# A gated S4 convolution kernel: weight products taken in the loaded layout and turned as sums, the lag rearrangement in 16 wider matmuls, residual matrices on GpSimd, and a new order of the work

## The chip, the core and the metric

The kernel runs on one core of one Trainium2 chip. TensorE (PE), VectorE (DVE), ScalarE (ACT), GpSimd (POOL) and SyncE (SP, which issues most of the DMAs) run side by side, each through its own instructions in a fixed order, and wait for one another through semaphores. The metric is the device time of one execution in microseconds; the time shown for a kernel is the median of its runs.

## What is computed

`A_u` is a sequence of 2048 tokens by 512 channels. Three things are done with it and mixed: a long convolution with a kernel that is a sum of 128 damped exponentials per channel (branch a), a small feed-forward network applied to the two tokens that a router picks (branch b), and a gate per token.

```python
def reference(...):
    def _A_ref(u, A_re, A_im, B_re, B_im, C_re, C_im, log_dt, Dskip):
        dt = jnp.exp(log_dt)[:, None]
        logdA = dt * (A_re + 1j * A_im)
        dB = dt * (B_re + 1j * B_im)
        l = jnp.arange(L).astype(bfloat16)                       # lags, rounded to bf16
        P = jnp.exp(logdA[:, :, None] * l[None, None, :])
        K = jnp.einsum("dn,dnl,dn->dl", C_re + 1j * C_im, P, dB).real
        y = irfft(rfft(K padded to 2 L) * rfft(u padded to 2 L))[:L]
        return y + u * Dskip
    def _B_ref(x, w_r, w_gate, w_up, w_down):
        idx = two tokens with the largest x @ w_r
        y = ((silu(x[idx] @ w_gate) * (x[idx] @ w_up)) @ w_down) * sigmoid(x[idx] @ w_r)
        return x with y added at the rows idx
    g = sigmoid((A_u * gate_w).sum(-1, keepdims=True))
    return g * _A_ref(A_u, ...) + (1 - g) * _B_ref(A_u, ...)
```

The weight of each exponential is the complex product C·B·dt. The parameter matrices are 512 channels by 128 exponentials (`N`).

## The kernel before

Nothing loops at run time: the program writes out some 570 steps, and each step has a name (`"kmm"`, `"sel"`, ...), one or more engines that it may run on (its *alternatives*, with a cost that the author's planner assumes), the buffers it reads and writes, and a number in the order in which it was written down. `PLAN` is a list of (step number, alternative) that fixes by hand which engine takes a step and the order on each engine; `BANKS` does the same for the places of the 83 PSUM tiles. `emit_plan` derives the semaphore waits. So an engine that waits for one step holds up everything behind it in its own list.

The 512 channels are worked on as two halves `hf` = 0, 1 (called `c` in later stages) of 256. The stages, with the names used below:

- **Weights.** Six parameter matrices are loaded as `NAT` (`nat0` to `nat5`), each with the channels in groups of four on the 128 partitions. `turned` (line 505) turns a matrix with four matmuls, so that the exponentials lie on the partitions: `nt0`, `nt1` for A, `nt2` to `nt5` for B and C. `cce` copies the turned C out of PSUM. `w1`, `w2`, `wr`, `wi` form the real and imaginary part of C·B, and `kw` multiplies by dt. `k0` sums `kw` for lag 0.
- **Coarse and fine factors.** Every lag is a sum of a coarse and a fine part. `ep` and `eq` are 256-wide exponentials on ACT (line 401), `pa` computes angles on PE (lines 578, 579), `arg` computes others on DVE or ACT (lines 559, 560), `sin` evaluates them on ACT, and `ns`, `pi`, `pr` (coarse) and `px` to `qr` (fine, `group`, line 794) multiply on DVE. The exponentials of half 0 that run first need only `al`.
- **Transform.** `fw` (line 724) multiplies the input tokens `U` (two loads of 1 MB, `u0`, `u1`) with Fourier matrices `FM`; `fwe` and `fwo` evict from PSUM, `vb` combines.
- **Lags** (line 842). `kmm` (line 853): 128 small matmuls per half give the convolution kernel at all lags; `kae` evicts them into `KA`. `sel` (line 868) brings the lags into the order that the next stage needs, as a product with selection matrices, 32 rows of output at a time, and `kce` evicts that into `KC`.
- **Spectrum** (line 874). `ks` (lines 886 to 891) multiplies `KC` with Fourier matrices, `khe` evicts; `i` = 0 is the near part of the lags, `i` = 1 the far part. Four tiles of `ks` per half and part, two PSUM banks each.
- **Products** (line 908). `prod`, `acc`, `yr`, `yi`, `pq` on DVE multiply the two spectra, for half `c` and output block `j`. For `c` = 0, `j` = 1 the sums are taken on PE instead (`ac`, line 936), which reads four `prod` results.
- **Inverse** (line 963). `iv` (lines 990, 993) transforms back and accumulates, per tile one matmul with a residual matrix `RD` that brings in branch b, `ive` multiplies by the gate on the way out of PSUM, and `out` stores.
- **Rows.** `log` gives router and gate values. The gate goes through the chain `sge` (ACT), `sgd` (POOL), `sgr` (DVE), `sgo`, `gf`, `gc`, `omg` (POOL); `rrec` (DVE) and `rr` (POOL) form (1 - g) / g per token, and `rd` (line 1043) multiplies the identity by it: eight 128x128 diagonal matrices per output block. `sc` (POOL) scatters the two rows of branch b into a copy of the input, and `ue` and `u2` load that copy back.

`TT` (line 375) is the helper of nearly all DVE products, `EV` (line 397) that of the evictions (ACT line 392 or DVE line 398), `AF` that of ACT functions (line 401).

Of the kernel before, what the change touches and what calls it, by code (L numbers as in the profile page):

```python
# [1121 lines left out]
```

## Time and profile before

| | us |
|---|---|
| median of 3 runs | 169.33 |
| lowest, highest run | 169.23, 172.55 |
| the profiled execution's own time | 168.66 |
| its span, first to last instruction | 166.9 |

The mean granted clock of TensorE was 0.98. The profile has a page with the busy time of each engine, the span in 40 slices, the chain of work that ended last and the costliest groups, and its trace can be asked for the instructions in order of time (the timeline: start, duration, engine, line, operation, output and input, number merged, idle time before and what ended it) and for busy times by window.

### The profile page before, as it was taken

The numbers are of one execution on the slowest core, as the hardware profiler recorded it, in microseconds if no ns is written. First come the engines' busy times: TensorE is split into PE (matmuls) and PEld (weight loads), VectorE is DVE, ScalarE is ACT, GpSimd is POOL, SyncE is SP. The second block draws the span as 40 slices with busy tenths as digits, with TensorE's granted clock in tenths as the row PEclk, the third lists the DMA queues.
The fourth block names the chain that finished last, engine by engine and source line by source line (L and its number), as shares of the span: only waits on it lengthen the run. The fifth ranks groups of instructions, "written<-read, shape, count | busy, mean of one in ns | idle before, by whom it ended". The sixth has DMA issues, their size and how long they took to land.

```text
span 166.9 us, 3538 instructions
## 1 busy us (share of the span) xinstructions
PE 149.1 (89%) x1483; PEld 108.0 (65%) x1491; DVE 146.0 (88%) x172; ACT 129.9 (78%) x243; POOL 17.9 (11%) x27
## 2 busy tenths in 40 slices
PE   1738998999999999999946899999999999999993
PEld 0523475666684685575633778768886785887882
DVE  0598899999998997898899999899897989999952
ACT  4599988999999999998999899698477360443432
POOL 6000000116005580000000042000000000000000
PEclk9975999999999999999999999999999999999999
DMA  3899999990009900001891000979300004001226
GB/s 113 300 356 230 265 389 374 415 377 18 1 9 335 602 4 0 4 0 29 277 401 51 2 4 24 338 298 370 110 0 0 4 0 126 0 4 55 70 70 181
DMA packets 21330, 25.89 MB, mean 155 GB/s; under 512 B 9118, under 2 KB 17188, under 8 KB 20644
## 3 DMA queue, kind: packets, MB, share of 16 engines
q1 hardware_dynamic: 21042, 25.55, 46.0%
q8 instruction: 11, 0.18, 0.4%
q10 hardware_dynamic: 146, 0.13, 0.2%
q0 software_dynamic: 128, 0.01, 0.2%
q14 instruction: 3, 0.02, 0.0%
HBM read 21.49 MB, written 4.20 MB: 154 GB/s over the span
## 4 chain that ended last, share of the span: by engine, by line
PE 62%; ACT 21%; DVE 7%; DMA 6%; SPq 2%; issue 1%
PE psm L993 17%; PE psm L724 12%; ACT RB L401 11%; PE psm L886 6%; ACT RB L392 6%; DVE RB L376 6%; DMA RB<-in_A_u_dram 6%; PE psm L936 4%; PE psm L853 3%; PE psm L578 3%; PE psm L579 3%; ACT L401 2%; PE psm L990 2%; PE psm L890 2%; PE psm L891 2%; PE psm L868 2%
## 5 line engine op out<-in xcount | busy, mean ns | idle before, releaser
L376 DVE TENSOR_TENSOR RB<-RB 128x2048 bf16<-128x2048 bf16 (+6 forms) x119 | 121.7, 1059 | 5.2 <-ACT RB L392 1.9
L392 ACT ACTIVATE RB<-psm 128x1024 bf16<-128x1024 f32 (+7 forms) x46 | 39.9, 908 | 12.3 <-PE psm L936 5.5
L401 ACT ACTIVATE RB<-RB 128x256 bf16<-128x256 f32 (+3 forms) x111 | 41.1, 452 | 2.3 <-DVE RB L376 2.3
L724 PE MATMUL psm<-RB 128*128 128x512 bf16 x121 | 31.7, 395 | 1.3 <-DMA RB<-in_A_u_dram 0.5
L993 PE MATMUL psm<-RB 128*128 128x256 bf16 x256 | 31.7, 273 | 0.0
L993 PEld LDWEIGHTS psm<-RB 128*128 128x128 bf16 x256 | 25.0, 98 | 3.1
L1007 ACT ACTIVATE RB<-psm,RB 128x256 bf16<-128x256 f32 x27 | 11.3, 472 | 16.6 <-PE psm L993 16.6
L401 ACT ACTIVATE RB<-psm 128x1024 bf16<-128x1024 int16 (+2 forms) x25 | 22.2, 936 | 0.6 <-PE psm L579 0.5
L724 PEld LDWEIGHTS psm<-RB 128*128 128x128 bf16 x128 | 12.6, 101 | 15.4 <-issue 2.2
L579 PE MATMUL psm<-RB 128*128 128x256 f16 x88 | 18.2, 273 | 0.3 <-ACT RB L401 0.3
L886 PE MATMUL psm<-RB 128*128 128x256 bf16 x128 | 16.3, 273 | 0.3 <-ACT RB L392 0.3
L578 PE MATMUL psm<-RB 128*128 128x256 f16 x88 | 15.0, 273 | 0.3 <-ACT RB L392 0.3
L853 PE MATMUL psm<-RB 128*128 128x80 bf16 x256 | 12.3, 199 | 2.5 <-ACT RB L392 1.6
L886 PEld LDWEIGHTS psm<-RB 128*128 128x128 bf16 x128 | 12.4, 98 | 2.1 <-ACT RB L392 0.6
L853 PEld LDWEIGHTS psm<-RB 128*128 128x128 bf16 x256 | 10.2, 97 | 4.9 <-PE psm L853 2.5
L401 ACT ACT_TABLE_LOAD x7 | 9.0, 1283 | 1.8 <-PEq L1107 1.7
L509 PE MATMUL psm<-RB 128*128 128x128 bf16 x24 | 5.4, 454 | 5.2 <-DMA RB<-in_A_B_re_dram 3.5
L578 PEld LDWEIGHTS psm<-RB 128*128 128x128 f16 x88 | 8.4, 98 | 2.5 <-ACT RB L392 0.4
L579 PEld LDWEIGHTS psm<-RB 128*128 128x128 f16 x88 | 8.2, 98 | 2.5 <-ACT RB L401 0.9
L398 DVE CAST RB<-psm 128x1024 bf16<-128x1024 f32 (+1 forms) x7 | 8.2, 1191 | 1.6 <-PE psm L853 1.1
L727 PE MATMUL psm<-RB 128*128 128x512 bf16 x31 | 9.3, 379 | 0.1
L990 PE MATMUL psm<-RB 128*128 128x256 bf16 x32 | 8.7, 273 | 0.2 <-issue 0.2
(64 smaller groups left out, 123.4 us busy)
## 6 DMA issues: line engine op xcount, KB each, us to landing
RB<-c_fwd SPq DMA_DIRECT2D x2, 1024.0 KB, 6.5
RB<-in_A_u_dram SPq DMA_DIRECT2D x2, 1024.0 KB, 9.4
RB<-c_near SPq DMA_DIRECT2D x2, 1024.0 KB, 5.1
RB<-c_inv SPq DMA_DIRECT2D x1, 2048.0 KB, 8.3
RB<-u_routed SPq DMA_DIRECT2D x2, 1024.0 KB, 6.8
RB<-in_B_w_gate_dram SPq DMA_DIRECT2D x1, 1792.0 KB, 9.9
RB<-in_B_w_up_dram SPq DMA_DIRECT2D x1, 1792.0 KB, 10.2
RB<-in_B_w_down_dram SPq DMA_DIRECT2D x1, 1792.0 KB, 7.5
```

Source lines behind the costliest of these rows:

```text
L376: return P.add(name, [(eng, c_dve(n, mode) if eng == DVE else 1.6, lambda h: h.tensor_tensor(out=o(), in0=a_(), in1=b_(), op=op))], rd, wr ...
L392: return lambda h: h.activation(out=o(), in_=a_(), func=ACTF.Copy, scale=scale() if callable(scale) else scale)
L401: return P.add(name, [(ACT, cost or c_act(n), lambda h: h.activation(out=o(), in_=a_(), func=func, scale=scale))], rd, wr, table=table, **kw)
L578: h.matmul(o, DGM(0, 128, (DPE.index(d) + 2) * 128, (1, 128)), HL(0, 128, k * 512 + c0, (1, w)), start=(k == 0 and i * w % 512 == 0), stop ...
L579: r = h.matmul(o, DGM(0, 128, 0, (1, 128)), DGM(0, 128, 128 + 1 - cs, (0, w)), start=False, stop=(cs == 0), skip_group_check=True)
L724: r = h.matmul(P32(t, k2, 0, 128, 0, (1, 512)), FM(0, 128, pl * 4096 + (par * 4 + q) * 512 + (2 * kp + k2) * 128, (1, 128)), U(0, 128, ((m ...
L727: r = h.matmul(P32(t, k2, 0, 128, 0, (1, 512)), CI(0, 128, 128 if pl == 1 - par * hc else 256, (1, 128)), V(0, 128, vo[0][2 * kp + k2] + ( ...
L853: x = h.matmul(P32(t, q // 6, 0, 128, (q % 6) * 80, (1, 80)), TPv(0, 128, ri * 16384 + c * 8192 + r * 128, (1, 128)), TQv(0, 128, c * 1024 ...
L886: x = h.matmul(o, KN(0, 128, g * 2048 + col, (1, 128)), KC[c](0, 128, g * 256, (1, 256)), start=(g == 0), stop=(g == NG - 1 and pl == 1))
L990: h.matmul(o, RD(0, 128, (tb + 8) % 16 * 128, (1, 128)), UE[qp](0, 128, (q2 * 2 + par) * 256, (1, 256)) if early else U2(0, 128, tb * D + ...
L993: x = h.matmul(o, G(0, 128, (pl * 4 + k0_ + kt) * 1024 + (par * 4 + q) * 128, (1, 128)), PQ(0, 128, 2048 * par + (k0_ + kt) * 512 + pl * 2 ...
L1007: r = h.activation(out=OT[k](0, 128, (4 * qp + 2 * q2 + par) * 256, (1, 256)), in_=P32(t, 0, 0, 128, q2 * 256, (1, 256)), func=ACTF.Copy, ...
```

## The change

- The turns `nt2` to `nt5` and `cce` go. `w1`, `w2` multiply the loaded bf16 matrices directly, `wr`, `wi` follow, and the two float32 sums are turned by eight transposes, a new PE step `wt`, into a two-bank PSUM tile that `kw` reads. `wt` needs the float32 identity `cf`.
- `sel` writes four PSUM banks, one for each remainder `c4`, each with all 320 columns in order, in 16 matmuls instead of 48; `kce` puts the order right as it reads: its innermost step goes from bank to bank.
- `rd` gets a third alternative, one GpSimd multiplication with an assumed cost of 4.5, and the plan takes it for both output blocks. Before, ACT made both.
- `PLAN` and `BANKS` are new throughout. SP's order becomes `nat5, cia, nat1, nat3, nat2, nat4, dgb, cf, dga, dsr, u0, fm, xt` (before: `cia, nat1, nat4, dga, nat3, nat5, fm, nat2, u0, xt, dgb, cf, dsr`). PE runs 24 `pa` matmuls and `wt` ahead of the first `fw`. Of the `arg` steps six go from ACT to DVE and one from DVE to ACT. From DVE to ACT go one `fwe`, one `fwo` and two wide `kae` of half 0; from ACT to DVE one `fwe`, one `ns` and the narrow `kae` of half 1. The gate's chain from `sge` to `rr`, which ran beside the coarse and fine stages, comes after `sc` on POOL, with `sge` on ACT among the evictions of the first spectrum and `rrec` on DVE behind the `yr` of the first products. `iv` of the first block, which stood in part between `sel` of half 1 and the second spectrum, comes wholly behind the first `ac`. On PE `zt` moves ahead of `sel` of half 0, and on DVE `bu` behind the last fine product. A few assumed latencies and priorities of loads, which only the planner reads, are changed as well.

```diff
-PLAN = [(0, 0), (4, 0), (5, 0), (3, 0), (6, 0), (1, 0), (23, 0), (29, 0), (225, 0), (2, 0), (13, 0), (7, 0), (180, 0), (22, 0), (244, 0), (207, 0), (243, 0),
...
+PLAN = [(0, 0), (14, 0), (3, 0), (4, 0), (5, 0), (1, 0), (23, 0), (6, 0), (24, 0), (234, 0), (242, 0), (240, 0), (203, 0), (2, 0), (22, 0), (25, 0), (26, 0),
...
-tB, tC = P.pst(2, "tb"), P.pst(2, "tc")
-for i in range(4):
-    turned(2 + i, (tB, tC)[i // 2], i % 2)
-CC = at("TP", 58880, 2048, BF); bCC = bf_("cc", "TP", 58880, 2048)
-EV("cce", row(CC, 0, 1024), lambda: P32(tC, 0, 0, 128, 0, (1, 1024)), [tC], [bCC], 1024)
...
-TT("w1", row(W1, 0, 1024), pq_(tB, 0, 1024), row(CC, 0, 1024), ALU.mult, [tB, bCC], [bW1], 1024, 1)
+TT("w1", row(W1, 0, 1024), lambda: NAT(0, 128, 1024, (1, 1024)), lambda: NAT(0, 128, 2048, (1, 1024)), ALU.mult, bNAT[2:], [bW1], 1024, 1)
...
+tW = P.pst(2, "tw")
+def wt(h):
+    r = None
+    for i, w in enumerate((W1, W2)):
+        for db in range(4):
+            r = h.transpose(P32(tW, i, 0, 128, db, (4, 128)), w(0, 128, db * 128, (1, 128)), CF(0, 128, 0, (1, 128)))
+    return r
+MM("wt", wt, [bW1, bW2, bCF], [tW], 2.0)
-TT("kw", row(KW, 0, 1024), lambda: W12(0, 128, 0, (1024, 2), (1, 512)), lambda: DTB(0, 128, 0, (0, 2), (1, 512)), ALU.mult, [bW1, bW2, bDTB], [bKW], 1024, 1)
+TT("kw", row(KW, 0, 1024), lambda: P32(tW, 0, 0, 128, 0, (1, 1024)), lambda: DTB(0, 128, 0, (0, 2), (1, 512)), ALU.mult, [tW, bDTB], [bKW], 1024, 1)
...
-t = P.pst(3, "sel")
+t = P.pst(4, "sel")
...
-    for jp in range(3):
-        nj = 2 if jp < 2 else 1
-        for c4 in range(4):
-            for g in range(4):
-                x = h.matmul(P32(t, jp, 32 * g, 32, c4, (256, nj), (4, 64)), CI(0, 128, 384 + 32 * c4, (1, 32)),
-                             KA[c](0, 128, (8 * jp + g) * 4 + c4, (16, nj), (80, 64)), start=True, stop=True, tile_position=(0, 32 * g))
+    for c4 in range(4):
+        for g in range(4):
+            x = h.matmul(P32(t, c4, 32 * g, 32, 0, (1, 320)), CI(0, 128, 384 + 32 * c4, (1, 32)),
+                         KA[c](0, 128, 4 * g + c4, (16, 5), (80, 64)), start=True, stop=True, tile_position=(0, 32 * g))
...
-EV("kce", lambda: KC[c](0, 128, 0, (1, 1280)), lambda t=t: P32(t, 0, 0, 128, 0, (1, 1280)), [t], [bKC[c]], 1280)
+EV("kce", lambda: KC[c](0, 128, 0, (256, 5), (4, 64), (1, 4)), lambda t=t: P32(t, 0, 0, 128, 0, (64, 5), (1, 64), (512, 4)), [t], [bKC[c]], 1280)
...
-             (ACT, 2.4, rd_act)], [bCIA, bSGF["rr"]], [bRD[j]])
+             (ACT, 2.9, rd_act), (POOL, 4.5, lambda h: h.tensor_tensor(out=RD(0, 128, (8 - 8 * j) * 128, (128, 8), (1, 128)), in0=CI(0, 128, 0, (0, 8), (1, 128)), in1=SGF["rr"](0, 128, 8 * j, (1, 8), (0, 128)), op=ALU.mult))], [bCIA, bSGF["rr"]], [bRD[j]])
```

15 lines of the change are left out of this document (7 added, 8 removed), and 74 rows, old and new, of the table PLAN.

## The prediction

> **What bounds the kernel now.** I read the page's busy times first, then its 40 slices, then busy times by window, and last the timeline of each engine around the hand-overs that these show.
>
> ```profile
> span 166.9 us, 3538 instructions
> PE 149.1 (89%) x1483; PEld 108.0 (65%) x1491; DVE 146.0 (88%) x172; ACT 129.9 (78%) x243; POOL 17.9 (11%) x27
> ...
> PE   1738998999999999999946899999999999999993
> ...
> DVE  0598899999998997898899999899897989999952
> ACT  4599988999999999998999899698477360443432
> ```
>
> No engine has much room, so the question is which of them sets the pace in which stage. PE dips in slices 21 and 22 only, ACT is full until about slice 25, and DVE is nearly full throughout.
>
> ```profile
> 5.86:92.30 86.44, 76.19 (x767) 48.36 (x773) 80.00 (x109) 84.45 (x164) 12.39 (x18) 0.96 0.63 209
> 92.30:103.70 11.40, 11.08 (x100) 9.45 (x101) 11.09 (x14) 10.86 (x23) 2.87 (x1) 1.00 0.01 2
> 103.70:127.20 23.50, 22.90 (x309) 19.07 (x307) 20.43 (x17) 17.41 (x26) 0.00 (x0) 1.00 0.57 202
> 127.20:166.90 39.70, 36.58 (x303) 29.18 (x300) 33.81 (x34) 15.35 (x30) 0.00 (x0) 1.00 0.19 54
> ```
>
> After each window's length stand PE, PEld, DVE, ACT, POOL, the clock and the DMA's share. In the first window ACT has 84.45 of 86.44 us: it sets the pace until `kce` of half 0. From there PE does (11.08 of 11.40, 22.90 of 23.50), with DVE close behind. The timeline shows the hand-overs:
>
> ```profile
> 85.90 1.27 PE L853 MATMUL psm<-RB 128*128 128x80 bf16 x24 [1.57 <-ACT RB L392]
> 88.23 2.69 PE L868 MATMUL psm<-RB 128*32 128x128 bf16 x48 [1.06 <-ACT RB L392]
> 92.31 0.28 PE L890 MATMUL psm<-RB 128*128 128x256 bf16 x1 [1.39 <-ACT RB L392]
> 92.43 0.27 PE L891 MATMUL psm<-RB 128*128 128x256 bf16 x1
> ...
> 103.71 6.17 PE L853 MATMUL psm<-RB 128*128 128x80 bf16 x128
> ...
> 113.71 0.28 PE L990 MATMUL psm<-RB 128*128 128x256 bf16 x1
> ...
> 115.69 0.27 PE L890 MATMUL psm<-RB 128*128 128x256 bf16 x1
> ...
> 93.29 0.38 PE L697 MATMUL psm<-RB 128*2 128x128 bf16 x4
> ...
> 95.50 2.43 ACT L1043 ACTIVATE RB<-RB 128x128 bf16<-128x128 bf16 x8
> ```
>
> `ks` starts at 92.31, when ACT has evicted `sel`. `kmm` of half 1 starts at 103.71, the first `ac` at about 127.2, the end of the third window. I move these marks.
>
> **The head.** The four turns, `cce` and their waits go:
>
> ```profile
> 4.48 9.27 DMA RB<-in_A_u_dram
> 7.66 1.23 DVE L398 CAST RB<-psm 128x1024 bf16<-128x1024 f32 x1 [0.52 <-PE psm L509]
> 11.13 2.13 PE L509 MATMUL psm<-RB 128*128 128x128 bf16 x8 [3.51 <-DMA RB<-in_A_B_re_dram]
> 29.43 0.49 PE L635 MATMUL psm<-RB 128*128 128x128 f32 x2
> ```
>
> On PE they lay in waiting time (3.51 us) and are worth nothing. `wt` is eight float32 turns; the nearest row is the float32 128x128 product, 0.49 us for one, so eight lie between 1 us (half of it, pipelined) and 3.9; I take 2. `wt` waits for `wi` and `wr`; behind it in PE's list stands the first `fw`, and DVE's `kw` waits for it with `arg` and both `fwo` queued behind. That costs DVE 1 to 3 us, about what it saves with `cce` (1.23) and its two waits on the turns. On SP some 650 KB (`dgb`, `cf`) now precede `u0`, which took 9.27 us for what was queued ahead: I add 2 us for `fw`, and the 24 `pa` matmuls that fill PE meanwhile (2.6 us at the 0.11 us spacing of 92.31 to 92.43) pay it back. ACT has its exponentials all this time, so this part is costed at nothing; if the exponentials ran out before `pa`, up to 2 us would show.
>
> **ACT to the first spectrum.** From ACT's groups within the first window:
>
> ```profile
> L401 ACT ACTIVATE RB<-RB 128x256 bf16<-128x256 f32 x98 | 31.2, 404 | 2.3 <-DVE RB L376 2.3
> ...
> L392 ACT ACTIVATE RB<-psm 128x1024 bf16<-128x1024 f32 x9 | 8.9, 1011 | 0.1
> ...
> L560 ACT ACTIVATE RB<-RB 128x512 int32<-128x512 f32 x7 | 4.1, 621 | 0.0
> L392 ACT ACTIVATE RB<-psm 128x960 bf16<-128x960 f32 x3 | 2.8, 964 | 0.1
> L392 ACT ACTIVATE RB<-psm 128x1280 bf16<-128x1280 f32 x1 | 1.2, 1219 | 0.0
> L392 ACT ACTIVATE RB<-RB 128x1024 bf16<-128x1024 bf16 x1 | 1.1, 1067 | 0.0
> ...
> L392 ACT ACTIVATE RB<-psm 128x32 f32<-128x32 f32 x1 | 0.2, 198 | 1.0 <-PE psm L615 1.0
> ```
>
> One starts about 0.1 us before the last has ended, so I count each mean less 0.1. Ahead of `kce` go five `arg` net (2.6), `ns` (0.97), two exponentials net (0.6) and half a microsecond of small steps; in come one eviction net (`fwe`, `fwo` in, a `fwe` out: 0.91) and two `kae` (1.73). Net 2.0 less. The first load (`nat5`) delays the first exponential by some 0.25, and `sel` with fewer steps around it may leave ACT waiting; I move `ks` 1.4 earlier, to 90.9 (bounds 0 to 3). `kce` from bank to bank has no row: the eviction in order is 1.22, I keep that and put double as its upper bound. PE then does what it did until 103.71 (11.4, of which `zt`, 0.3 on line 697, has moved ahead): `kmm` of half 1 starts at 102.0. DVE's fine products end before that: they ended at 103.3, and DVE is rid of about 3 us (`cce`, two evictions, two `kae` against six `arg`, one eviction).
>
> **PE and DVE to the first `ac`.** PE: 23.5 as before, less the early `iv` (113.71 to 115.69, 1.98), which used to cover `kce` of half 1; without it the second spectrum waits for `kce`, 1.3. `sel`'s columns:
>
> ```profile
> L868 PE MATMUL psm<-RB 128*32 128x128 bf16 x32 | 2.2, 432 | 1.1 <-ACT RB L392 1.1
> L868 PE MATMUL psm<-RB 128*32 128x64 bf16 x16 | 0.7, 311 | 0.0
> ```
>
> Half the columns, about half the busy time (0.07 us against 0.04 for each), so the cost is by columns, not by matmuls, and 16 x 320 columns are as many as 32 x 128 + 16 x 64. I take 0.2 off 2.69; the other bound is 0.55, four times 320 columns at the 0.11 us for 256 of `ks`. PE stands ready for `ac` at 102.0 + 23.5 - 1.98 + 1.3 - 0.2 = 124.6.
>
> DVE must wait for the narrow `kae`, so for the end of `kmm`: 102.0 + 6.2 = 108.2.
>
> ```profile
> 103.20 4.48 DVE L376 TENSOR_TENSOR RB<-RB 128x4096 bf16<-128x4096 bf16 x2
> 108.77 1.16 DVE L398 CAST RB<-psm 128x960 bf16<-128x960 f32 x1 [1.08 <-PE psm L853]
> 109.84 10.55 DVE L376 TENSOR_TENSOR RB<-RB 128x2048 bf16<-128x2048 bf16 x9
> ```
>
> A third of that `kae` is 0.4; then come one large product (2.24), `rrec` (0.2) and ten others of 1.17: `vb`, `yr`, `yi`, two `pq`, five `prod`. The `prod` that `ac` needs ends at 108.2 + 0.4 + 2.24 + 0.2 + 11.7 = 122.8, before PE wants it. But `rr` and both `rd` now run on POOL in just this stretch, since `rr` follows `rrec`, at about 113.5.
>
> ```profile
> 28.14 0.19 POOL L376 TENSOR_TENSOR RB<-RB 128x1 f32<-128x1 f32 x1 [24.55 <-DVE RB L636]
> 64.92 0.22 POOL L376 TENSOR_TENSOR RB<-RB 128x16 f32<-128x16 f32 x1 [2.88 <-DVE RB L706]
> ...
> 58.29 1.18 DVE L376 TENSOR_TENSOR RB<-RB 128x2048 bf16<-128x2048 bf16 x1
> 58.43 1.09 POOL L386 CAST RB<-RB 128x16 bf16<-128x16 f32 x1 [2.00 <-DVE RB L625]
> ...
> 3.03 0.56 POOL L532 MEMSET RB<- 128x512 bf16 x1
> ```
>
> 15 more elements cost 0.03 us, 2.1 ns each: 1024 take 0.19 + 2.15 = 2.35. (Lower bound 1.1, twice the 512-element memset; upper 4.5, which the diff itself books.) And the cast of 16 elements, which began while DVE's product ran, took 1.09 us and ended at 59.52, 0.05 after the product (59.47): POOL had stood still until DVE was done. If they exclude each other, DVE stands still while POOL holds on: 2 x 2.35 = 4.7. Then `ac` starts at 122.8 + 4.7 + 0.1 = 127.6. From there 39.7 as before and the `iv` put off, 1.98, together 41.7: the span is 169.3.
>
> [...]
>
> ACT's diagonal copies, twice eight in 2.43 us, free an engine that has 6 us to spare in the third window: nothing. The other queue effect, `sc` ahead of the gate's chain on POOL (2.87 us in the second window), ends before `rrec`.
>
> **The rivals.** *No exclusion, or slack that hides it:* `ac` starts when PE is ready, 124.6, and the span is 124.6 + 41.7 = 166.3, 0.6 less than now. For it: no row shows DVE held up for long. Its far end is a cheap `sel`: if the old one is slow because it writes every fourth column, the new one, in order, takes 0.55. PE is then ready at 122.6, DVE at 122.9, the span is 164.6. [...] Against it: the cost by columns fits strided reading as well, which stays.
>
> [...] At 4.5 us each `ac` starts at 122.8 + 9.0 + 0.1 = 131.9 and the span is 173.6. It decides from about 3 us for one (span 170.5). For it: the 4.5 that the diff books, and that the one POOL row beside DVE took 1.09 us for 16 elements; against it, that row can be the waiting alone.
>
> *The wider `sel` saves nothing* is my forecast's own term; it costs 0.2 a half.
>
> **The numbers.** The profiled execution took 168.66, 1.76 more than its span, and the median is 0.67 above it. I sum against the profiled one, adding 1.76 to each span: forecast 171.0; rivals 168.0 (down to 166.3) and 175.3. Chances: 0.38 the forecast (its own range 169 to 173.5, from `ks` 1.5 sooner or later and `kce`), 0.30 no exclusion, 0.32 longer holding, with other stalls of the new order in it. About 2% is what a measurement of this kernel can tell from no change: 165.9 and 172.7 about the median. Faster takes 0.18 of the second case (cheap `sel`, or ACT's gap of 1.0 at `log`, line 615, closed too), slower the third and 0.1 of the first; 0.40 stay within. The range goes from 166.3 less 1 us for that gap to 175.3 less nothing plus half of a doubled `kce`: 165.3 to 176.
>
> **What would show it.** Right: two POOL rows of about 2.3 us on 128x1024, DVE rows on two SBUF inputs stretched or idle beside them, PE idle for 2 to 3 us ahead of the first matmul of line 936, `ks` near 91. Wrong: DVE rows of 1.2 us beside POOL's; a `sel` of 0.6 us; `ks` later than 92.3, which would put the loss into the head or ACT's order.

## The result, and the profile after

The changed kernel takes 1.006 of the time before, with a 95% interval of 1.003 to 1.009: about 1 us slower. The profiled execution took 170.37 us, where 171.0 was forecast, with a span of 168.4. The two profiled executions lie 1.7 us apart (168.66 and 170.37), so differences read from the two profiles come out somewhat larger than the ratio. In 12 of its 20 runs the changed kernel took 172.7 to 173.3 us at a lower granted clock (0.97), so its median is 172.83; all ratios here leave such runs out, but three profiles below (`rd` back on ACT, `rd` made twice, the last `ks` moved) are of such a run.

| mark, us | before | forecast | after |
|---|---|---|---|
| first `fw` | 13.79 | 2 later | 14.97 |
| `ks` of half 0 starts | 92.31 | 90.9 | 91.81 |
| `kmm` of half 1 starts | 103.71 | 102.0 | 102.31 |
| PE's wait for `kce` of half 1 | covered | 1.3 | 1.35 |
| PE ready for the first `ac` | 127.2 | 124.6 | 125.1 |
| first `ac` starts | 127.2 | 127.6 | 126.64 |
| from there to the end | 39.7 | 41.7 | 41.76 |
| span | 166.9 | 169.3 | 168.4 |

First the page of the changed kernel: busy times, then the 40 slices.

```profile
span 168.4 us, 3385 instructions
...
PE 148.8 (88%) x1419; PEld 104.6 (62%) x1419; DVE 147.9 (88%) x175; ACT 124.5 (74%) x223; POOL 25.6 (15%) x29
...
PE   2369999998998999987956999969979999999993
...
DVE  0699899999996899879899998699999989999962
ACT  4699999999969999999987996852764231624432
POOL 6000000150482030000100007308700000000000
```

ACT is rid of 5.4 us, POOL has 7.7 more, and DVE is busier than before (147.9 against 146.0), though about 3 us of work were taken from it. The windows cut at the same marks as before show where (length, then PE, PEld, DVE, ACT, POOL, clock):

```profile
5.52:91.81 86.29, 76.43 (x742) 47.18 (x740) 78.80 (x110) 82.91 (x157) 11.61 (x12) 0.96 0.65 221
91.81:102.30 10.49, 10.49 (x96) 9.30 (x96) 10.11 (x13) 10.16 (x19) 0.03 (x1) 1.00 0.31 134
102.30:126.64 24.34, 21.04 (x259) 16.14 (x257) 22.26 (x18) 14.37 (x15) 11.20 (x9) 1.00 0.34 109
126.64:168.40 41.76, 38.90 (x320) 30.96 (x320) 36.02 (x36) 15.15 (x32) 0.00 (x0) 1.00 0.18 51
```

In the first window ACT worked 82.91 us instead of 84.45, yet the window is only 0.15 shorter. In the third PE, which had been idle for 0.6 us, is idle for 3.3. The timeline of PE names its waits, and below it stand DVE and POOL in the third window:

```profile
87.82 2.65 PE L868 MATMUL psm<-RB 128*32 128x320 bf16 x16 [1.61 <-ACT RB L392]
91.81 0.61 PE L886 MATMUL psm<-RB 128*128 128x256 bf16 x4 [1.34 <-ACT RB L392]
113.58 0.28 PE L890 MATMUL psm<-RB 128*128 128x256 bf16 x1 [1.35 <-ACT RB L392]
126.64 1.90 PE L936 MATMUL psm<-RB 128*128 128x512 bf16 x8 [1.53 <-DVE RB L376]
```

```profile
113.93 2.44 DVE L376 TENSOR_TENSOR RB<-RB 128x2048 bf16<-128x2048 bf16 x2
115.26 2.86 POOL L1046 TENSOR_TENSOR RB<-RB 128x1024 bf16<-128x1024 bf16 x1
116.29 2.92 DVE L376 TENSOR_TENSOR RB<-RB 128x2048 bf16<-128x2048 bf16 x1
115.26 5.70 POOL L1046 TENSOR_TENSOR RB<-RB 128x1024 bf16<-128x1024 bf16 x2
119.24 2.80 DVE L376 TENSOR_TENSOR RB<-RB 128x2048 bf16<-128x2048 bf16 x1
121.96 2.35 DVE L376 TENSOR_TENSOR RB<-RB 128x2048 bf16<-128x2048 bf16 x2
```

The two `rd` on POOL (a row with x2 merges two) stand beside DVE products of 2.92 and 2.80 us; the products before and after them take 2.44 and 2.35 for two. Read in order of time, these rows look like work in turns. The first `rd` begins at 115.26, and DVE's product beside it ends at about 116.37 (113.93 + 2.44); the `rd` ends at 118.12, 1.75 us after that, which I read as the time that it holds DVE up, and DVE's product, begun at 116.29, is done at 119.21. Then the same once more. The two products lose 2.92 + 2.80 - 2 x 1.21 = 3.3 us, and PE waits 1.53 us ahead of `ac`. That POOL is the cause is tested by the first four experiments.

### The profile page after: what moved, and what is told of

The parts are those of the page before. It is cut to its first block, busy times and chain, and to the rows that moved or that the text cites. A ratio compares the mean times of both kernels' runs of the same rounds, so it can differ in the third digit from the quotient of the medians.

```text
span 168.4 us, 3385 instructions
## 1 busy us (share of the span) xinstructions
PE 148.8 (88%) x1419; PEld 104.6 (62%) x1419; DVE 147.9 (88%) x175; ACT 124.5 (74%) x223; POOL 25.6 (15%) x29
## 4 chain that ended last, share of the span: by engine, by line
PE 53%; ACT 27%; DVE 15%; DMA 1%; issue 1%; ACTq 0%; DVEq 0%
ACT RB L401 20%; PE psm L993 17%; DVE RB L376 13%; PE psm L726 8%; PE psm L855 6%; ACT RB L392 5%; PE psm L886 4%; PE psm L936 4%; PE psm L729 3%; PE psm L990 2%; PE psm L868 2%; PE psm L580 2%; ACT L401 2%; DMA RB<-in_A_A_re_dram 1%; PE psm L581 1%
## 5 line engine op out<-in xcount | busy, mean ns | idle before, releaser
L376 DVE TENSOR_TENSOR RB<-RB 128x2048 bf16<-128x2048 bf16 (+5 forms) x120 | 125.9, 1089 | 3.7 <-ACT RB L401 1.0
L392 ACT ACTIVATE RB<-psm 128x1024 bf16<-128x1024 f32 (+7 forms) x47 | 42.8, 945 | 20.9 <-PE psm L936 8.3
L401 ACT ACTIVATE RB<-RB 128x256 bf16<-128x256 f32 (+2 forms) x111 | 41.1, 453 | 2.0 <-DVE RB L376 2.0
L726 PE MATMUL psm<-RB 128*128 128x512 bf16 x128 | 32.5, 392 | 0.9 <-ACT RB L392 0.7
L993 PE MATMUL psm<-RB 128*128 128x256 bf16 x256 | 31.8, 273 | 0.1
L1007 ACT ACTIVATE RB<-psm,RB 128x256 bf16<-128x256 f32 x27 | 10.8, 475 | 15.6 <-PE psm L993 15.6
L580 PE MATMUL psm<-RB 128*128 128x256 f16 x88 | 16.2, 288 | 3.9 <-DVE RB L376 3.5
L581 PE MATMUL psm<-RB 128*128 128x256 f16 x88 | 19.0, 280 | 0.3 <-ACT RB L401 0.3
L886 PE MATMUL psm<-RB 128*128 128x256 bf16 x128 | 16.2, 273 | 1.3 <-ACT RB L392 1.3
L729 PE MATMUL psm<-RB 128*128 128x512 bf16 x32 | 9.5, 379 | 0.0
L936 PE MATMUL psm<-RB 128*128 128x512 bf16 x32 | 7.4, 380 | 1.5 <-DVE RB L376 1.5
L990 PE MATMUL psm<-RB 128*128 128x256 bf16 x32 | 8.7, 273 | 0.0
L890 PE MATMUL psm<-RB 128*128 128x256 bf16 x32 | 7.3, 273 | 1.3 <-ACT RB L392 1.3
```

What stands on the lines that cost most here:

```text
L376: return P.add(name, [(eng, c_dve(n, mode) if eng == DVE else 1.6, lambda h: h.tensor_tensor(out=o(), in0=a_(), in1=b_(), op=op))], rd, wr ...
L392: return lambda h: h.activation(out=o(), in_=a_(), func=ACTF.Copy, scale=scale() if callable(scale) else scale)
L401: return P.add(name, [(ACT, cost or c_act(n), lambda h: h.activation(out=o(), in_=a_(), func=func, scale=scale))], rd, wr, table=table, **kw)
L580: h.matmul(o, DGM(0, 128, (DPE.index(d) + 2) * 128, (1, 128)), HL(0, 128, k * 512 + c0, (1, w)), start=(k == 0 and i * w % 512 == 0), stop ...
L581: r = h.matmul(o, DGM(0, 128, 0, (1, 128)), DGM(0, 128, 128 + 1 - cs, (0, w)), start=False, stop=(cs == 0), skip_group_check=True)
L726: r = h.matmul(P32(t, k2, 0, 128, 0, (1, 512)), FM(0, 128, pl * 4096 + (par * 4 + q) * 512 + (2 * kp + k2) * 128, (1, 128)), U(0, 128, ((m ...
```

## The experiments

All ratios are to the kernel before, run beside each. In three kernels (`rd` back on ACT, made twice, and in the kernel before) the order is written on one line, so that their line numbers are 36 or 37 lower (L339 is `TT`, L899 `ac`, L816 `kmm`, L1009 and L1010 `rd`); in others they are off by two or three.

### What `rd` on GpSimd costs: four kernels

**Back on ACT.** In `PLAN`, with its numbers:

```diff
-(99, 0), (390, 0),
+(99, 0), (50, 0), (100, 0), (390, 0),
...
-(465, 0), (510, 0),
+(465, 0), (326, 1), (510, 0),
...
-(467, 0), (50, 0), (100, 0), (469, 0), (326, 2), (527, 0), (440, 2),
+(467, 0), (469, 0), (527, 0), (440, 1),
```

> The changed kernel with both residual matrices back on ACT (eight diagonal copies each, among the second spectrum's evictions). If the two GpSimd multiplications shut DVE out (1.7 + 1.6 us of stretch, of which 1.53 show as PE's wait ahead of the first ac): the DVE products of 2048 columns all take 1.2 us again, ac starts where PE is ready, near 125.1 instead of 126.64, and the time falls by about 1.5 us, so 0.99 of the changed kernel and about level with the kernel before. If DVE's long products have another cause, or PE's wait does: they stay, and the time stays within 0.3 us.

Measured 0.9989 (0.9955 to 1.0023): 0.7% or 1.2 us below the changed kernel, near the 1.5. DVE's products in this stretch, and the first `ac`:

```profile
L339 DVE TENSOR_TENSOR RB<-RB 128x2048 bf16<-128x2048 bf16 x11 | 12.8, 1215 | 0.1
...
127.82 1.89 PE L899 MATMUL psm<-RB 128*128 128x512 bf16 x8
```

All take 1.2 us, and PE has no wait ahead of `ac`: its row names none. (It starts at 127.82 and not near 125.1, because this profiled execution, of 171.52 us, is late from the first spectrum on; the reason comes with the turned lags below.) But ACT's order changed here as well, so the next kernel changes less.

**On DVE itself**, at the same places of the order:

```diff
-(326, 2), (527, 0), (440, 2),
+(326, 0), (527, 0), (440, 0),
```

> The changed kernel with both residual matrices on DVE itself, at the places in its order which they had beside GpSimd; the products that ac needs come before them. If GpSimd takes the time from DVE: DVE does them for less than the 3.3 us that it stood still (near 0.7 to 1.2 each), ac starts at PE's readiness near 125.1, and the time falls by 0.5 to 1.5 us. If GpSimd takes nothing from DVE: DVE gets 1.4 to 2.4 us of work more while it is nearly full (12.36 of 13 us after 127), and the time stays or rises by up to 1.3 us.

Measured 1.0014 (0.9972 to 1.0055), 0.8 us below the changed kernel, though the two intervals overlap. The groups of DVE in that stretch, and the first `ac`:

```profile
L376 DVE TENSOR_TENSOR RB<-RB 128x2048 bf16<-128x2048 bf16 x13 | 15.2, 1218 | 0.5 <-ACT RB L392 0.4
L1045 DVE TENSOR_TENSOR RB<-RB 128x1024 bf16<-128x1024 bf16 x2 | 2.4, 1220 | 0.0
...
127.63 1.89 PE L936 MATMUL psm<-RB 128*128 128x512 bf16 x8
```

One `rd` takes DVE 1.22 us, less than the 1.65 that it lost to each on POOL. DVE does more instructions and the kernel is not slower for it, and PE's wait ahead of `ac` is gone.

**Each made twice on GpSimd**, the cost doubled:

```diff
-P.add("rd", [(DVE, ...
+for q in range(2):
+    P.add("rd", [(DVE, ...
```

> The changed kernel with each residual matrix made twice in a row on GpSimd (the second writes the same values again). If GpSimd's hold is taken out of DVE's time: two more DVE products of 1.2 us stretch to 2.8 to 2.9, ac starts 3.3 to 3.5 us later, near 130, the time rises by as much, to about 1.02 of the changed kernel. If the hold is not what delays ac: no change, since no one waits for the residual matrices until iv.

Measured 1.0381 (1.0332 to 1.0429), so 1.032 of the changed kernel, more than the 1.02 expected. The first lines are DVE's and POOL's, the last PE's:

```profile
116.81 18.32 DVE L339 TENSOR_TENSOR RB<-RB 128x2048 bf16<-128x2048 bf16 x10
118.14 11.36 POOL L1010 TENSOR_TENSOR RB<-RB 128x1024 bf16<-128x1024 bf16 x4
132.91 3.60 PE L899 MATMUL psm<-RB 128*128 128x512 bf16 x8 [4.92 <-DVE RB L339]
```

PE's wait grew from 1.53 to 4.92, by 3.39: what the theory said. Behind that wait the eight `ac` matmuls took 3.60 us instead of 1.90, and from `ac` to the end it was 44.2 us (177.1 less 132.91) instead of 41.76: PE came back at half its pace. Together these are 5.8 us, near the 5.4 between the two ratios. The profiled execution took 179.02 us, where the ratio rests on 175.8 to 176.6: it is 2.9 us late already where these products begin (116.81 against 113.93), which the edit doesn't touch. None of the theories had the half pace; it comes up again below.

**In the kernel before**, both `rd` on GpSimd and nothing else:

```diff
+             (POOL, 4.5, lambda h: h.tensor_tensor(...)),   # third alternative of rd
-(330, 1), ... (444, 1),
+(330, 2), ... (444, 2),
```

> The kernel before with both residual matrices on GpSimd, nothing else changed. If GpSimd shuts DVE out: one or both fall among the last fine products of half 1 (92 to 104 us), where DVE had 11.09 of 11.40 us of work, two of those products grow by about 1.7 us each, kmm of half 1 starts 1.5 to 3.5 us later and the time rises by 1.5 to 3.5 us (1.01 to 1.02 of the kernel before). If it does not: ACT is rid of 4.9 us that it had to spare, and the time stays or falls by up to 0.5 us.

Measured 1.015 (1.0105 to 1.0195), 2.5 us, inside the range.

```profile
101.85 2.73 DVE L339 TENSOR_TENSOR RB<-RB 128x1024 bf16<-128x1024 bf16 x1
102.11 1.91 POOL L1009 TENSOR_TENSOR RB<-RB 128x1024 bf16<-128x1024 bf16 x1
106.24 1.92 PE L816 MATMUL psm<-RB 128*128 128x80 bf16 x36 [1.89 <-DVE RB L339]
```

A product of 0.69 us took 2.73, and PE waited 1.89 for it ahead of `kmm` of half 1. Only one of the two `rd` fell among these products; the other ran at 65.46, where a product of 0.38 us took 1.21. So this part costs in the old order as well, where it meets DVE work close to the path.

### What the wider `sel` is worth, and what it could be: five kernels

**The old form in the changed kernel:**

```diff
-x = h.matmul(P32(t, c4, 32 * g, 32, 0, (1, 320)), ..., KA[c](0, 128, 4 * g + c4, (16, 5), (80, 64)), ...)
+x = h.matmul(P32(t, jp, 32 * g, 32, c4, (256, nj), (4, 64)), ..., KA[c](0, 128, (8 * jp + g) * 4 + c4, (16, nj), (80, 64)), ...)
```

> The changed kernel with the old lag rearrangement (48 narrow matmuls of 128 or 64 columns, written at every fourth column) and the old eviction in order, all else the same. If sel costs by its columns and the eviction does not mind changing banks: sel takes 2.69 instead of 2.64 us, kce 1.22 instead of 1.24, the time stays within 0.2 us. If the wider form hides a cost (the low granted clock of 0.61 beside it) or a gain: more than 0.5 us one way or the other.

Measured 1.0058 (1.0022 to 1.0095), the same as the changed kernel; `sel` took 2.69 and PE's three waits were 1.61, 1.34 and 1.34, as in the changed kernel. This part brings and costs nothing that the intervals, some 0.35% to either side, could show. (The low granted clock, 0.62 from 88 to 92 us, stands beside the old form too, at 0.66.)

**Reading in order:**

```diff
-KA[c](0, 128, 4 * g + c4, (16, 5), (80, 64))
+KA[c](0, 128, 320 * (4 * g + c4), (1, 320))
```

> The changed kernel in which sel reads 320 neighbouring columns of KA instead of five blocks of 64 columns, so that the lags come out in another order and the result is not the reference's; only sel's own duration is looked at. If the cost by columns (0.62 us for four matmuls of 320) comes from the blocks of the reading: sel takes about 0.55 us instead of 2.64. If it comes from something else (32 rows of output, or the columns themselves): sel stays at 2.6, and the old form's writing at every fourth column was not its cost either.

The expectation describes the reading loosely: it goes in steps of 80 elements, 64 times, for each of five blocks. Measured: `sel` of half 0 took 1.03 us instead of 2.65, and that of half 1, where the granted clock was 1.00 and not mostly 0.50, 0.73. So most of its cost is the reading, not the number of columns.

**Lags turned on the way out of PSUM.** `kae` writes in the order in which `sel` reads; residual matrices on ACT:

```diff
-dims = ((512, 2), (1, 480)) if nq == 12 else ((1, nq * 80),)
-EV("kae", ... KA[c](0, 128, (r0 + q0) * 80, (1, nq * 80)), ...
+dims = ((512, 2), (1, 80), (80, 6)) if nq == 12 else ((1, 80), (80, nq))
+EV("kae", ... KA[c](0, 128, r0 + q0, *(((6, 2), (64, 80), (1, 6)) if nq == 12 else ((64, 80), (1, nq)))), ...
-x = h.matmul(..., KA[c](0, 128, 4 * g + c4, (16, 5), (80, 64)), ...)
+x = h.matmul(..., KA[c](0, 128, 64 * (4 * g + c4), (1024, 5), (1, 64)), ...)
```

> The changed kernel with both residual matrices on ACT and the lags written by kae in the order in which sel reads them: kae reads PSUM in steps of 80 and writes runs of six, sel reads 64 neighbouring columns at a time. If the steps of 80 elements in sel's reading are its cost, and kae minds its steps as little as kce does (1.24 against 1.22): sel takes about 1.0 us instead of 2.65 in both halves. Of the first 1.6 us only about 0.7 shows, as DVE's fine products end at 101.6 and kmm of half 1 starts at 102.3; of the second all 1.6, as DVE has the products for ac at about 122.8. Sum 2.3 us below the kernel that has only the residual matrices on ACT, 0.985 of the kernel before. If kae slows down by as much in its place (up to twice 0.97 for each of four evictions on ACT): no gain or a loss.

Measured 0.9926 (0.9885 to 0.9966): faster than both kernels, by half of what was expected. `kae` minds its new steps not at all (0.974 us on ACT, 0.969 in the changed kernel). PE, and a window of it (length, then PE, PEld, DVE, ACT, POOL, clock):

```profile
88.54 0.73 PE L868 MATMUL psm<-RB 128*32 128x320 bf16 x16 [1.61 <-ACT RB L392]
91.49 1.03 PE L886 MATMUL psm<-RB 128*128 128x256 bf16 x4 [2.23 <-ACT RB L392]
```

```profile
91.49:96.40 4.91, 4.91 (x24) 3.48 (x25) 4.70 (x5) 3.27 (x10) 0.00 (x0) 0.50 0.87 370
```

`sel` takes 0.73, 1.9 less than before. In half 1 nearly all of it arrives: from `kmm` to the second spectrum 9.57 us (113.98 less 104.41) instead of 11.27. In half 0 less does. The wait for `kce` grew from 1.34 to 2.23, because `kce` stands behind six exponentials in ACT's queue, which `sel` used to outlast. And the first 24 matmuls of `ks` took 4.91 us, 0.21 each, at a granted clock of 0.50; in the changed kernel's profile they take 0.11 each.

That half pace is not shown to come from the turn: the profile with `rd` on ACT alone, where `sel` takes 2.65, has it too. The first line is `ks` of half 0 there, the second `ac` with the lags turned:

```profile
92.86 1.04 PE L849 MATMUL psm<-RB 128*128 128x256 bf16 x4 [1.34 <-ACT RB L355]
125.46 1.90 PE L936 MATMUL psm<-RB 128*128 128x512 bf16 x8
```

Between these two profiles, which both have half pace behind `sel`, `kmm` of half 1 starts 0.78 us earlier (105.19 to 104.41), the first `ac` 2.36 (127.82 to 125.46), and the span is 2.3 shorter (169.6 to 167.3): the 0.7, and the 2.3 in all, that were expected, in one execution of each. The 0.7 is luck, for PE at half pace and not DVE sets `kmm` there. The ratio with `rd` on ACT alone rests on executions at a granted clock of 0.98 and 0.99, that of this kernel mostly on 0.97; this may be why only half the gain shows between the ratios, but it was not tested.

**The queue put right,** `kce` behind two exponentials instead of six:

```diff
-(416, 0), (323, 0), (410, 0), (426, 0), (406, 0), (409, 0), (407, 0), (306, 0),
+(416, 0), (306, 0), (323, 0), (410, 0), (426, 0), (406, 0), (409, 0), (407, 0),
```

> The changed kernel with both residual matrices on ACT, the lags written in sel's order, and kce of half 0 moved in ACT's order from behind six exponentials to behind two, since sel now ends 1.9 us earlier than it did and kce stood behind exponentials until the end of the wait of 2.23 us. If that queue is what holds the first spectrum: the wait shrinks to 1.34, ks starts 0.9 us earlier (near 90.6) and the time falls by about 0.9 us against the same kernel without the move, to 0.987 of the kernel before; if PE's shorter idle time also keeps it at full pace (0.11 us for a matmul of 256 columns, where the first twenty took 0.21), by 2 us more. If DVE's fine products, which wait for the exponentials put off, set kmm of half 1: no gain.

Measured 0.9954 (0.993 to 0.9979), where the kernel without the move has 0.9926: no gain, though the shorter wait came as expected.

```profile
90.90 1.04 PE L886 MATMUL psm<-RB 128*128 128x256 bf16 x4 [1.35 <-ACT RB L392]
91.19 3.75 DVE L376 TENSOR_TENSOR RB<-RB 128x2048 bf16<-128x2048 bf16 x3 [1.88 <-ACT RB L401]
104.24 6.40 PE L855 MATMUL psm<-RB 128*128 128x80 bf16 x128
```

`ks` starts 0.6 us earlier and `kmm` of half 1 0.17 earlier, without a wait in between: PE ran at half pace until 96.6, where it had been 96.4. DVE does wait for the exponentials put off (1.88), but PE, not DVE, set `kmm`.

**The same turn in the kernel before,** `kae` writing as above and `sel` still in 48 matmuls that write every fourth column:

```diff
-KA[c](0, 128, (8 * jp + g) * 4 + c4, (16, nj), (80, 64))
+KA[c](0, 128, 64 * ((8 * jp + g) * 4 + c4), (1024, nj), (1, 64))
```

> The kernel before with the lags written in the order in which sel reads them, sel itself still 48 narrow matmuls that write every fourth column. If only the reading costs: sel takes about 1.0 us instead of 2.69, of which 0.4 (ahead of kmm of half 1, where DVE is close behind) to 1.7 us show at the first place and up to 1.7 at the second: the time falls by 0.5 to 2 us. If the writing at every fourth column costs as well: sel stays at 2 us or more and the time within 0.5.

Measured 1.0116 (1.0063 to 1.017), slower, which neither theory had. `sel` of half 1 took 1.28 us (not 0.73, so the old form costs 0.55 in itself once the reading is right, by its writing or by its 48 pieces), that of half 0 2.33 at a granted clock of 0.50, and behind it 19 matmuls of `ks` were 0.21 apart:

```profile
L886 PE MATMUL psm<-RB 128*128 128x256 bf16 x64 | 9.5, 299 | 0.0
```

In the profile before this mean is 273. From `ks` to `kmm` of half 1 it was 13.36 us instead of 11.40. Half pace had come once already, at 51.5 to 54.5, and ACT waited 1.26 us for PE behind it, in two waits. Whether the turn brings the half pace about was not separated.

### The weights and the head: two kernels

**The new weights alone in the kernel before** (order kept, `cf` loaded ahead of `xt`, `wt` behind the second `fw`):

```diff
-nt2 to nt5, cce; w1, w2 from PSUM and CC
+w1, w2 from NAT; wt; kw from PSUM
```

> The kernel before with the new weights alone: the turns of B and C and cce go, w1 and w2 take the loaded matrices, eight transposes turn the sums behind the second fw, and cf is loaded ahead of xt for them; order else as before. If this part costs and brings nothing (the forecast's term, zero): the first fw stays near 13.8, ks of half 0 stays at 92.3 within 0.3, the time within 0.5 us of the kernel before. If the part is a gain in itself (1.2 us less of DVE, PE's turns gone): up to 1.2 us faster. If the transposes between the fw, or the load ahead of xt, hold up the head: 1 to 2 us slower, to be seen at ks.

Measured 1.0072 (1.0041 to 1.0104), 1.2 us slower. PE in the head of this kernel, and ACT's wait for the router's matmuls:

```profile
13.35 6.48 PE L726 MATMUL psm<-RB 128*128 128x512 bf16 x16 [7.21 <-DMA RB<-in_A_u_dram]
19.66 1.04 PE L529 MATMUL psm<-RB 128*128 128x128 f32 x8
20.53 3.62 PE L726 MATMUL psm<-RB 128*128 128x512 bf16 x16
...
27.08 0.20 ACT L392 ACTIVATE RB<-psm 128x32 f32<-128x32 f32 x1 [2.53 <-PE psm L617]
```

Two things cost. The eight transposes stand between the `fw` and take 0.87 us (19.66 to 20.53). And without the turns PE had nothing to do for 7.21 us; of the 16 `fw` behind that wait 13 were 0.427 us apart, the other half take 0.216 each. In the kernel before eight were (seven and nine in two other profiles with this head). The 32 `fw` end 1.66 later, ACT, which waits for `log` behind them, waits 2.53 instead of 1.04, and `ks` of half 0 starts at 94.71 instead of 92.31: the head is on the path through that wait.

**The turns kept as work that nobody reads:**

```diff
+tB, tC = P.pst(2, "tb"), P.pst(2, "tc")
+for i in range(4):
+    turned(2 + i, (tB, tC)[i // 2], i % 2)
```

> The kernel before with the new weights, and the four turns of B and C kept on PE as work that nobody reads. With the new weights alone the 16 fw that follow PE's wait of 7.2 us are 0.40 us apart; with the turns still in the wait, in the kernel before, only eight were. If PE's pace after a wait is what the new weights alone cost: eight fw at 0.43 again, then 0.216, ks of half 0 1 to 1.6 us earlier, and the time 0.8 to 1.2 us lower, about level with the kernel before, though it does strictly more work than the new weights alone. If the loss came from the transposes between the fw or from cf ahead of xt: no change.

Measured 1.0065 (1.0035 to 1.0095): no change, so this explanation is not borne out by the time.

```profile
13.91 5.95 PE L729 MATMUL psm<-RB 128*128 128x512 bf16 x16 [0.46 <-DMA RB<-in_A_u_dram]
```

Eleven `fw` were still at half pace, though PE had worked up to 13.9 as in the kernel before, and `fw` started 0.56 later than without the turns. The transposes in line remain (0.87 us). Full pace came back at 17.2 us in the kernel before, at 18.8 here and at 19.2 without the turns; what sets this moment was not found.

### A wait covered: one kernel

**The last far `ks` of half 0 behind `sel` of half 1** (with the residual matrices on ACT):

```diff
-(455, 0), (317, 0), (457, 1), (168, 0), (48, 0), (458, 0), (318, 0),
+(455, 0), (457, 1), (168, 0), (48, 0), (458, 0), (317, 0), (318, 0),
```

> The changed kernel with both residual matrices on ACT and, besides, the last far ks of half 0 (eight matmuls, 0.9 us) moved behind sel of half 1, where PE waits 1.35 us for kce. If the put-off iv lost its cover there: that wait shrinks to about 0.5, ac can start 0.9 us earlier than with the residual matrices alone on ACT, near 124.2 if DVE has its products ready (122.8 by the forecast's sum), and the time is about 0.9 us below that kernel, so below the kernel before. If DVE is the bound at that place: PE's wait only moves to ac and the time stays.

Measured 1.0065 (1.0014 to 1.0117), not below the kernel with `rd` on ACT. PE's waits:

```profile
112.27 2.65 PE L868 MATMUL psm<-RB 128*32 128x320 bf16 x16 [0.86 <-ACT RB L392]
118.14 0.28 PE L890 MATMUL psm<-RB 128*128 128x256 bf16 x1 [2.24 <-ACT RB L392]
```

The moved matmuls had covered another wait, that of `sel` for `kae` (0.86 now). And in ACT's order the eviction of the moved `ks` still stood ahead of `kce`, so `kce` waited for it and PE for `kce`, 2.24 us. The edit was wrong: a step was moved on PE and its eviction was not moved on ACT. Whether DVE would have been the bound stays open.

## Why the prediction was right

The direction came out, and the time lies near the forecast partly by luck, because errors of the terms made up for each other. The forecast was 2.3 us more for the profiled execution (171.0 against 168.66); it took 1.7 more, and by the ratio the change costs 1.0.

- **The exclusion** of POOL and DVE was the forecast's main term, and it is shown: undone twice (0.7% less, and 0.5% less with overlapping intervals), doubled (PE's wait 3.39 longer), and put alone into the kernel before (1.5% more). The rival without exclusion falls, and so does the one of a longer hold: no run shows its 4.5 us a piece, one `rd` lasted 2.86 us, and 1.75 of them were hold. The term was mis-sized: 2.35 us a piece from 2.1 ns an element, measured 1.75 of hold (3.3 us in two products, not 4.7). By itself this would have put `ac` 1.4 earlier than forecast; it came 1.0 earlier, as DVE got to its products 0.4 later than summed.
- **ACT to the first spectrum** failed as a sum: `ks` came 0.5 us earlier, not 1.4. The work taken off was counted roughly rightly (1.54 us less busy up to `ks`, 2.0 expected). What was missed are ACT's waits. Those in the profile after:

```profile
47.11 1.02 ACT L392 ACTIVATE RB<-psm 128x1024 bf16<-128x1024 f32 x1 [0.58 <-PE psm L726]
48.86 1.94 ACT L401 ACTIVATE RB<-psm 128x1024 bf16<-128x1024 int16 x2 [0.73 <-PE psm L581]
85.94 1.83 ACT L392 ACTIVATE RB<-psm 128x960 bf16<-128x960 f32 x2 [0.80 <-PE psm L855]
90.52 1.24 ACT L392 ACTIVATE RB<-psm 128x1280 bf16<-128x1280 f32 x1 [0.92 <-PE psm L868]
```

These are 3.03 us; before, it waited 1.04 for `log` and 0.54 for `pa`, 1.58. The difference, 1.45, is what the sum lacked. (ACT's first exponential came 0.34 earlier, 5.52 instead of 5.86, where 0.25 later was forecast.) The last two waits, 1.72, belong to a chain in which `kmm`, `kae`, `sel`, `kce` and `ks` hand over between PE and ACT one after the other, so that less work on ACT no longer shortens it. The first two, 1.31, stand behind eight `fw` that ran at half pace, in 3.32 us. In the changed kernel with the old `sel`, which has the same order, these `fw` ran at full pace, the two waits are not there, and `ks` starts at 91.42:

```profile
44.74 1.90 PE L726 MATMUL psm<-RB 128*128 128x512 bf16 x8 [0.28 <-ACT RB L392]
```

Of the 0.9 that `ks` came late against the forecast, 0.6 was made good by `kmm` of half 1: between them lie 10.5 us, not 11.1, in part because a wait of PE for ACT (0.31 us, at 98.89 before) did not come again.
- **`sel` by its columns** was right for this way of reading, 2.65 against 2.5; **`kce` from bank to bank** costs nothing (1.24 against 1.22). The rival with a cheap `sel` came near the price (0.55 as its bound, 0.73 measured with the lags turned) and had the cause wrong: steps of 80 elements in the reading make most of it (2.65 us with them, 0.73 without), and the old form itself 0.55 (1.28 against 0.73).
- **The head at nothing** was right as a net, not as argued. `wt` lies in PE's wait in the new order and took 1.1 us, not 2; `fw` began 1.2 later, not 2 (1.5 to 2.2 later in the eight other profiles with this head, where the `pa` stayed at half pace longer). By 22.2 us PE had done the 32 `fw`, 24 `pa` and `wt`, where before it had done the `fw` alone by 22.3. In the old order the same weights cost 1.2 us, so the `pa` and `wt` in the wait seem to pay for them, as forecast; this is argued, as no run moves the `pa` alone. Behind them `fw` runs at full pace from its first matmul:

```profile
9.69 0.61 PE L580 MATMUL psm<-RB 128*128 128x256 f16 x2 [3.49 <-DVE RB L376]
...
13.75 1.09 PE L529 MATMUL psm<-RB 128*128 128x128 f32 x8
14.97 3.63 PE L726 MATMUL psm<-RB 128*128 128x512 bf16 x16
```

- **The `iv` put off**: its cover was missed as forecast (1.35 for 1.3) and it cost what it takes (41.76 for 41.7).

So, between the two profiles, the change gains 1.4 us up to `kmm` of half 1 (103.71 to 102.31), gives 1.35 away at `kce` and 1.53 at `ac`, and the `iv` only changes its place: 1.98 less ahead of `ac`, 2.06 more behind it. That is 1.5 us of span in all, 166.9 to 168.4. With `rd` on ACT it is level with the kernel before (0.9989): the new order and the new weights are worth nothing measurable together, and the loss is the part on GpSimd.

## What to carry to other kernels

Giving `rd` to GpSimd did not take work off a busy DVE here: beside DVE's products it cost DVE 1.65 us a piece, where DVE itself does it in 1.22, so look who is at work on DVE at the time. When an engine is rid of work, add up its waits anew, above all along a chain that goes to and fro between two engines, and look in each queue at what stands ahead of the step that is to come sooner. The same eight `fw` took 3.32 us in one profile here and 1.90 in another of the same order, so compare profiles that are alike in pace before a gain or a loss behind a changed step is put down to the step.

## What had not been expected of the hardware

PE's matmuls ran at half pace in stretches; where the granted clock shows them, it is 0.50: for 3.41 us in the changed kernel (43.25 to 46.66 and 87.62 to 91.03), for 6.82 in the kernel before (10.29 to 17.11) and in the one with `rd` on ACT (89.81 to 96.63). The spacing of matmuls of 256 columns is then 0.213 instead of 0.109 us, of 512 columns 0.427 instead of 0.216. In the changed kernel this hit the `pa` behind a wait of 3.49 us (9.69 to 12.6) and eight `fw` behind the narrow matmuls of the router's branch:

```profile
41.92 1.56 PE L674 MATMUL psm<-RB 128*128 128x2 bf16 x56 [0.65 <-ACT RB L392]
43.75 3.32 PE L726 MATMUL psm<-RB 128*128 128x512 bf16 x8 [0.27 <-ACT RB L392]
```

It comes at `sel` of half 0 too. The windows of the changed kernel and of the one with `rd` on ACT (length, then PE, PEld, DVE, ACT, POOL, clock):

```profile
87.62:91.03 3.41, 2.65 (x16) 0.42 (x16) 2.97 (x3) 2.49 (x8) 0.00 (x0) 0.50 1.07 437
...
89.81:96.63 6.82, 5.48 (x30) 2.84 (x23) 6.58 (x6) 4.97 (x13) 0.00 (x0) 0.50 0.98 410
```

In the changed kernel the half clock lies on `sel` and the wait behind it and is over before `ks` starts at 91.81. In the other it lasts twice as long, and `ks` pays for it. `ks` was hit so in eight profiles of this study: `rd` on ACT, on DVE, made twice, the last `ks` moved, the reading in order, and the three with the lags turned. In the first four `sel` took 2.65 us as in the changed kernel, so a shorter `sel` is not needed for it. In six of the eight it ended at 96.2 to 96.8 us, though `ks` began anywhere from 90.90 to 92.86; in the other two at 95.5 and 98.8. So in these eight it did not end after a fixed number of matmuls, and starting sooner won little (0.6 us sooner for `ks`, 0.17 for `kmm` of half 1, with `kce` put right). `sel` in steps of 80 did not mind: it took 2.65 us at 0.50 in half 0 and at 1.00 in half 1.

No long idle time of PE stands ahead of the stretch that begins at 87.62: in the 3.41 us before it PE was at work for 1.89, and its longest wait, up to 87.82, was 1.61. The granted clock of the windows shows most of it but not all: at 9.69 to 12.60 it says 1.00 while the matmuls are 0.213 apart. What brings it about, and what decides how long it lasts and so whether `ks` is hit, was not separated here.
